# A long-convolution and gated-MLP kernel on one core: two transfers for the first rows, a shorter warm-up, and a new written-out order

## The chip, the cores and the metric

The kernel runs on one core of a Trainium2 chip. The metric is the device time of one execution in microseconds (us). TensorE (PE in the profile, its weight loads PEld), VectorE (DVE), ScalarE (ACT), GpSimd (POOL) and SyncE (SP, which here issues most DMAs) run side by side and wait for each other by semaphores.

## What is computed

All tensors are bfloat16, with 2048 rows of 512 columns. A layer norm of q feeds two branches, whose product is added to q:

```python
x  = A_q
xn = layernorm(x)                       # over the 512 columns
# branch A: shifted k, times v, long convolution over the 2048 rows, times xn
k_shift = sum over t in 0..3 of k_pad[:, t:t+S, :] * shift_k[:, 3-t]
kv = k_shift * v
y  = irfft(rfft(pad(kv)) * rfft(pad(ssm_k)))[:S] + kv * ssm_D
s  = xn * y
# branch B: gated MLP, 512 -> 1792 -> 512
h  = gelu(xn @ w_gate) * (xn @ w_up)
g  = silu(h @ w_down)
return x + s * g
```

## The kernel before

The 2048 rows are 16 tiles of 128 (tile t holds every sixteenth row), and four quarters q of four tiles.

**The MLP.** `ln` (L806 to L818) normalises a quarter: statistics on DVE, a power of -0.5 on POOL, XN written by DVE. `xn_transpose` (L839 for quarters 0 and 1, by matmuls against an identity on PE and copies out of PSUM at L593 or L596; L831 for quarters 2 and 3, by a DMA) makes xnT. `unit(q, m)` multiplies xnT by 128 columns of Wg and of Wu, 14 units to a quarter (matmuls at the helper's L602); ACT applies gelu into GE (L1063, L1072), DVE multiplies into HT (L1065, L1075). The first two units of quarter 0 work in halves of 256 columns, so that they can begin with two of four tiles. Wg and Wu arrive in four parts each, for 2, 4, 4 and 4 of the 14 units (`load_w`). `down(q)` multiplies HT by Wd, 14 matmuls to a tile. In the last quarter ACT applies silu (L1107), DVE multiplies by s and adds x (L1109, L1110), and the tile is stored. The very last tile, t = 15, is cut into two pieces of columns, so that the first is finished while the second is computed.

**The convolution** is a Fourier transform of length 4096 in two stages, by matmuls with tables. The filter ssm_k (Hn) is transposed on PE (L863, f32 view), copied to HTr, multiplied by the table F1 and stored to DRAM (ZH); D is added to one row of HTr (L877). k and v are combined on DVE in four quarters (`kshift`, L940 to L948; the result stands in V), multiplied by F1 and stored (ZK). Both come back as BH and BK for the second stage, whose matmuls are 32x32 tiles (L963). Products of spectra (L1026), the inverse stage (L963, HS and HW with MI), a store (ZI), a load (BI) and a last matmul follow.

**The order.** The program does not run in the order in which it is written down. Each step is a task, with the buffers that it reads and writes; `Sched.run` goes through the tasks in the order of `SEQ`, a list of task numbers written out by hand in the file (a `b` behind a number takes the step's second engine). Every engine executes its share strictly in that order and waits by semaphores for what it needs. `Sched.run` keeps estimated times (`LOAD_NS` for loads, `pe`, `act`, `dve` for the engines), by which it picks free buffers; PSUM has eight banks, of which four may be held by MLP matmuls, four by transposes, and pairs by the convolution. `ORDER` is the order in which load tasks are numbered.

**The start.** `warm_up` issues N_WARM matmuls on a tile of zeros (AST, cleared at L655) into a PSUM bank that nobody reads. SP's queue begins with D (1 KB, L574 like all its copies), four loads of one tile of X each (128 rows of 1 KB per tile), two parts of Hn, Wg's and Wu's first parts, the second quarter of X, Wg's second part, the rows of k that overlap, and so on.

Of the kernel before, what the change touches and what calls it, by code (L numbers as in the profile page):

```python
# [14 lines left out]
DM = 512  # L15
FF = 1792
NT = 16
# [2 lines left out]
NQ = 4  # L20
NG = 32
LN_EPS = 1e-5
TURN = 8192
N_WARM = 22
ORDER = "x00 x01 x02 x03 w0 w1 h0 h1 h2 h3 D0 w2 s0 k0 v0 x1 w3 k1 v1 d0 d1 k2 v2 k3 v3 x2 x3"
SEQ = (
    "28 19 0 2 18 10 3 17 16 4 24 25 11 73 71 1 5 7 6 8 72 50 67 74 79 69 68 20 70 9 21 80 37 75 22 12 82 51 87 81 52 86 32 76 26 23 78 77 54 90 91b "
    "85 89 27 33 84 88 55 367 359 14 53b 356 56 355 357 369 441 439 358 13 363 368 360 361 57 362 379 364 127 381 365 128 440 443 366 442 375 97 377 "
    "98 371 122 444 370 380 59 373 123 61 445 376 446 63 447 58 448 112 15 65 382 450 451 452 378 60b 31 35 34 133 132 134 135 38 383 113 129 384 130 "
    "114 385 115 131 136 449 137 39 30 29 36 45 40 41 372 374 138 62 403 124 407 64 66 386 415 408 125 405 409 99 453 416 395 455 139 410 140 417 418 "  # L30
    "126 100 116 457 459 399 454 456 141 404 102 144 397 47 44 46 42 43 101 460 458 103 401 142 391 400 406 402 145 117 396 119 392 387 393 118 107 "
    "388 398 143 120 389 108 146 390 147 394 104 411 94 485 105 106 413 487 148 465 109 149 412 152 150 414 467 92 110 111 93 95 419 466 477 211 420 "
    "96 212 121 479 216 217 486 218 421 219 422 151 153 488 154 423 155 468 228 461 226 463 227 493 229 156 495 462 429 469 213 434 464 214 157 158 "
    "494 430 221 496 159 160 220 49 230 431 223 222 176 168 215 171 432 224 471 161 162 435 231 505 236 507 433 232 237 83 478 424 233 470 425 163 "
    "234 225 48 235 480 164 165 472 166 481 436 489 238 167 437 491 483 426 490 427 239 473 492 241 475 438 428 630 541 628 539 242 246 474 247 243 "
    "506 248 497 169 170 240 476 629 482 244 542 631 484 245 508 632 634 633 635 636 249 172 499 173 637 174 501 509 498 503 177 500 250 502 513 511 "
    "178 179 515 510 514 641 504 639 638 640 517 181 175 251 182 264 518 183 186 277 180 537 512 516 538 543 540 522 252 544 253b 545 523 546 254 184 "
    "519 256 520 265 255 269 266 549 547 257 548 521 258 532 524 525 527 278 642 185 282 279 290 191 526 267 268 550 533 528 259 262b 260 270 271 529 "
    "534 187 530 263 261 531 188 659 647 535 661 649 651 653 189b 272 275 273 551 655 652 648 280 281 303 190 283 284 285 196 654 650 663 274 657 286 "
    "643 288b 291 536 292b 287 665 295 656 660 658 662 192 644 572 645 193b 646 588 664 194 574 666 293 304 294 296 701 556 589 573 590 308 305 558 "  # L40
    "197 198 199 575 297 591 584 552 195 554 585 298 586 306 299 316 301 592 557 580 307 309 587 559 317 593 201 329 200 206 553 321b 709 555 276 289 "
    "318 582 202 594 203 204 604 319 310 595 596 581 311 300 606 598 302 320 583 322 605 600 568 597 323 607 599 312 314 324 560 564 205 327b 342 602 "
    "325 570 326 328 566 330 334 565 331b 569 576 207 567 571 332 333 578 208 209 562 210 577 691 601 579 335 336 603 561 337 671 713 563 315 340 673 "
    "338b 705 695 618 343 344 693 341 347b 345 346 697 692 619 348 349 608 696 609 698 694 350 339 351 613 683 620 352 353b 354 685 621 313 687 614 "
    "726 715 610 615 707 611 689 616 684 686 622 612 617 623 667 624 668 625 672 669 626 627 674 727 675 716 679 728 670 717 711 699 723 708 729 688 "
    "681 677 718 772 710 680 690 682 676 700 712 678 724 736 730 703 773 719 702 764 714 768 725 770 721 704 743 737 720 738 731 739 744 750 722 706 "
    "757 745 740 732 766 733 774 741 734 769 765 771 746 735 775 767 742 747 751 758 752 753 759 748 754 755 749 760 761 762 756 763 "
)
NF_BANKS = 4
ISSUE = 470.0  # L50
LOAD_NS = {131072: 400.0, 262144: 900.0, 524288: 1300.0, ("h", 524288): 1700.0, ("wg", 524288): 1500.0, ("wu", 524288): 1500.0, 917504: 2620.0, ("sk", 524288): 1900.0, 344064: 1100.0, 46080: 200.0, 3072: 100.0, 1024: 50.0}
W_XT, W_SW, W_BK, W_BH, W_ZI, W_BI, W_ZK, W_MI, W_G1 = 1665000, 600000, 555000, 703000, 333000, 640000, 490000, 740000, 222000
NC_PAIRS = 4
SMALL = 1.15 * 262144
# [235 lines left out]
class Sched:  # L290
# [7 lines left out]
    SHARE_BW = 300.0  # L298
    FIRST = {"loads": 300.0, "SP": 30500.0}
    DRAIN = 121.0  # L300
    EARLY, TAKEN, SHARED, WAIT = (2400.0, 1.3), 1200.0, 46000.0, 3300.0

    def __init__(self):
        self.tasks = []
# [37 lines left out]
    def run(self):  # L342
        free = dict(self.FIRST)
        pipe = 0.0
        order = []
        pmode = 0
        for name in SEQ.split():
            t = self.tasks[int(name.rstrip("b"))]
            eng, dur = t.opts[name[-1] == "b"]
            base = 0.0  # L350
            for d in t.deps:
                base = max(base, d.end + d.lat + (self.SEM if not d.nbytes or t.opts[0][0] != "PE" else 400.0 if d.eng == "loads" else self.HEDGE))
            for b in t.w:
                if b.pool is not None and b.slot is None:
                    f, b.slot = b.pool.find()
                    b.pool.take(b.slot)
                    base = max(base, f + self.SEM)
            t.start, t.eng = max(base, free.get(eng, 800.0)), eng
            free[eng] = t.end = t.start + dur + (self.DRAIN if eng == "PE" and t.mode != pmode else 0.0)
            pmode = t.mode if eng == "PE" else pmode  # L360
            if eng == "loads":
                free[eng] = t.start + dur * (self.EARLY[1] if t.start < self.EARLY[0] else 1.0)
                t.end = free[eng] + self.LOAD_LAT
            elif t.nbytes:
                en = t.end
                if en < self.SHARED:
                    free["loads"] += self.TAKEN
                pipe = max(pipe, en + self.DMA_LAT / 2) + t.nbytes / (self.SHARE_BW if en < self.SHARED else self.DMA_BW)
                t.end = pipe + self.DMA_LAT / 2 + (self.WAIT if en < self.SHARED else 0.0)
            for b in set(t.r + t.w):  # L370
                b.left -= 1
                b.last_end = max(b.last_end, t.end + t.lat)
                if b.left == 0 and b.pool is not None:
                    b.pool.release(b.slot, b.last_end)
            order.append(t)
        assert sorted(t.n for t in order) == list(range(len(self.tasks)))
        return order


def pe(n, cols=512):  # L380
    return n * (cols / 2.4 + 3.0)
# [10 lines left out]
def build_kernel(nc, A_q, A_k, A_v, A_shift_k, A_ssm_k, A_ssm_D, B_w_gate, B_w_up, B_w_down, out):  # L392
    with ExitStack() as es0:
# [19 lines left out]
        X = new("X", [128, NT, DM], BF16)  # L413
# [23 lines left out]
        G = new("G", [128, NT, DM], BF16)  # L437
# [53 lines left out]
        S = Sched()  # L491
        res = trk.res
# [15 lines left out]
        R_X = [res(f"X{t}", X[:, t, :]) for t in range(NT)]  # L508
# [11 lines left out]
        R_GE = [res(f"GE{j}", GE[:, j, :]) for j in range(3)]  # L520
        R_AST = {x: [res(f"AST{x}{j}", a) for j, a in enumerate(ast[x])] for x in "HK"}
        R_G = [res(f"G{t}", G[:, t, :]) for t in range(NT)]
        R_Gh = [res(f"Gh{i}", G[:, NT - 1, 256 * i:256 * i + 256]) for i in range(2)]
        R_HT = [[res(f"HT{j}_{m}", HT[:, j, m, :]) for m in range(MF)] for j in range(2)]
        R_KK = [res(f"KK{t}", KK[:, t, :]) for t in range(19)]
        R_kz = res("kz", KK[0:1, 0:3, :])
# [88 lines left out]
        bWd = [B(f"Wd{i}") for i in range(2)]  # L615
# [43 lines left out]
            for i in range(N_WARM):  # L659
                trk.op("PE", lambda h: mm(h, bank(warm), ZERO[:, 0:128], ZERO, True, True), r=[R_zero], w=R_bank(warm), accum=True)  # L660

        t_warm = S.add([("PE", 10 * 390.0 + (N_WARM - 10) * 220.0)], warm_up, r=[bwarm], w=[warm])
        bcq, bck, bid32 = B("cq"), B("ck"), B("id32")
        S.add([("POOL", 370.0)], lambda e: pool_q(), w=[bcq])
        S.add([("POOL", 1080.0)], lambda e: pool_k(), w=[bck])
# [90 lines left out]
            x_late.append(S.add([("SP", ISSUE)], lambda e: dma(e, args[0], args[1], sem, [], args[2]), w=args[3], nbytes=480000, after=last_load))  # L756

        def load_x0(t, ring):
            load(f"x0_{t}", X[:, t, :], x_dr[:, t, :], R_X[t:t + 1], [bX[0][t]], 131072, ring)

        def load_w(i, rings=("SP", "SP")):
            f0, n = FC[i]
# [315 lines left out]
        def down(q):  # L1078
            for jt in range(4):
                t = 4 * q + jt  # L1080
                cols = [(0, DM)] if t < NT - 1 else [(0, DM // 2), (DM // 2, DM)]
                for c0, c1 in cols:
                    p = B(f"psd{q}_{jt}_{c0}", pF)

# [3 lines left out]
                    for m0, m1 in ((0, 4), (4, 9), (9, 14)):  # L1088
                        def f(e, p=p, jt=jt, m0=m0, m1=m1, pc=pc, c0=c0, c1=c1):
                            for m in range(m0, m1):  # L1090
                                trk.op("PE", lambda h, m=m: mm(h, pc(), HT[:, q % 2, m, 128 * jt:128 * (jt + 1)], Wd[:, m, c0:c1], m == 0, m == MF - 1),
                                       r=[R_HT[q % 2][m], R_Wd[m // 7]], w=R_bank(p), accum=True)
                        down_tasks[q].append(S.add([("PE", pe(m1 - m0, c1 - c0))], f, r=(bHT[q] if jt else bHT[q][m0:m1]) + bWd[m0 // 7:(m1 + 6) // 7],
                                                   w=[p], lat=200.0))
                    n = c1 - c0
                    g, rg = G[:, t, c0:c1], [R_G[t] if n == DM else R_Gh[c0 // n]]
                    bt = B(f"tanh{q}_{jt}")
                    if q < NQ - 1:
                        op([("ACT", act(n))], lambda e, h, g=g, pc=pc: h.activation(g, pc(), ACTF.Tanh, scale=0.5), r=[p], w=[bt],  # L1099
# [122 lines left out]
```

## Time and profile before

| | us |
|---|---|
| median of 3 runs | 198.84 |
| lowest, highest | 198.42, 199.41 |
| the profiled execution | 199.92 |
| its span, first to last instruction | 198.1 |
| PE busy | 192.3 (97% of the span) |
| DVE busy | 159.2 (80%) |
| ACT busy | 122.7 (62%) |
| POOL busy | 12.7 (6%) |

A matmul's busy time overlaps with the next one's, so a PE that is busy throughout still has a pace, which is read from the distance of starts. The span begins with the first instruction and ends with the last; the time of an execution holds some 1.8 us more around it. The chain of waits follows the work that ended last back to its beginning, and at each step names what released it. DMA share is the mean busy share of the 16 DMA engines.

### The profile page before, as it was taken

The page shows a single profiled execution, that of the slowest core. Times are in us where ns is not written, and L with a number is a line of the kernel's source. Part 1 is how long each engine was busy: PE and PEld are TensorE (multiplying, and loading weights), DVE is VectorE, ACT ScalarE, POOL GpSimd, SP SyncE. Part 2 cuts the span into 40 slices and gives each one's busy share as a digit, 9 for nine tenths or more (in the row PEclk, how much of TensorE's full clock was granted, in tenths as well). Part 3 has the DMA queues.
Part 4 walks back from the last instruction along what each step waited for, and adds up shares of the span by engine and source line. Part 5 has one row for each costly group of instructions (what it writes and reads, how often), then busy time and mean ns, then how long its engine had stood idle before and what let it go on. Part 6 is the DMA issues. An engine that isn't in the chain of part 4 may idle for free.

```text
span 198.1 us, 3524 instructions
## 1 busy us (share of the span) xinstructions
PE 192.3 (97%) x1396; PEld 88.2 (45%) x1396; DVE 159.2 (80%) x245; ACT 122.7 (62%) x166; POOL 12.7 (6%) x26
## 2 busy tenths in 40 slices
PE   7998999999999999999999999999999999999993
PEld 2584555444444444444334334434343444444452
DVE  6678898999899995897789796878698815499783
ACT  2587797877883797985667867878654334140031
POOL 6300730000000000020200000000000000000000
PEclk9999999999999999999999999999999999999999
DMA  4999999997759835798999927777512348387406
GB/s 125 346 292 348 366 377 414 416 387 255 303 184 285 294 107 159 237 342 262 311 309 251 378 92 255 265 231 230 192 56 109 106 162 314 113 245 228 160 2 212
DMA packets 34790, 48.14 MB, mean 243 GB/s; under 512 B 8403, under 2 KB 27735, under 8 KB 34774
## 3 DMA queue, kind: packets, MB, share of 16 engines
q1 hardware_dynamic: 29270, 39.53, 61.2%
q10 hardware_dynamic: 5504, 8.39, 11.5%
q8 instruction: 11, 0.18, 0.4%
q14 instruction: 5, 0.04, 0.1%
HBM read 27.39 MB, written 14.68 MB: 212 GB/s over the span
## 4 chain that ended last, share of the span: by engine, by line
PE 90%; DMA 5%; SPq 2%; ACT 1%; DVE 1%; issue 0%
PE psall L602 83%; PE psall L963 5%; DMA Wg<-in_B_w_gate_dram 5%; SPq L574 2%; PE psall L863 1%; ACT HTr L593 1%; PE psall L839 0%; DVE G L1110 0%; DVE G L1109 0%; ACT G L1107 0%
## 5 line engine op out<-in xcount | busy, mean ns | idle before, releaser
L602 PE MATMUL psall<-xnT,Wg 128*128 128x512 bf16 (+1 forms) x232 | 55.6, 372 | 1.0 <-DMA Wg<-in_B_w_gate_dram 1.0
L602 PE MATMUL psall<-xnT,Wu 128*128 128x512 bf16 (+1 forms) x232 | 56.3, 372 | 0.0
L602 PE MATMUL psall<-Wd,HT 128*128 128x512 bf16 (+1 forms) x238 | 53.5, 367 | 0.0
L1075 DVE TENSOR_TENSOR HT<-psall,GE 128x512 bf16<-128x512 f32 x54 | 36.6, 687 | 17.7 <-PE psall L602 16.7
L1072 ACT ACTIVATE GE<-psall 128x512 bf16<-128x512 f32 x54 | 31.1, 600 | 16.9 <-PE psall L602 15.2
L602 PEld LDWEIGHTS psall<-Wd,HT 128*128 128x128 bf16 x238 | 22.8, 98 | 25.6 <-issue 1.3
L602 PEld LDWEIGHTS psall<-xnT,Wg 128*128 128x128 bf16 x232 | 21.8, 98 | 26.9 <-issue 2.2
L602 PEld LDWEIGHTS psall<-xnT,Wu 128*128 128x128 bf16 x232 | 22.0, 98 | 25.3 <-issue 1.8
L593 ACT ACTIVATE HS<-psall 128x1024 bf16<-128x1024 f32 x14 | 13.7, 1021 | 4.9 <-PE psall L963 4.8
L593 ACT ACTIVATE BO<-psall 128x1024 bf16<-128x1024 f32 x11 | 10.9, 1022 | 8.6 <-PE psall L963 8.6
L946 DVE TENSOR_TENSOR KAC<-KAC,KTM 128x2048 bf16<-128x2048 bf16 x12 | 14.6, 1219 | 0.1
L944 DVE TENSOR_TENSOR KTM<-KK,SKB 128x2048 bf16<-128x2048 bf16 x12 | 14.6, 1217 | 0.1
L593 ACT ACTIVATE KB<-psall 128x1024 bf16<-128x1024 f32 x11 | 10.9, 1022 | 4.6 <-PE psall L963 4.6
L593 ACT ACTIVATE AST<-psall 128x1024 bf16<-128x1024 f32 x10 | 10.2, 1025 | 4.5 <-PE psall L602 4.5
L1107 ACT ACTIVATE G<-psall 128x512 bf16<-128x512 f32 (+1 forms) x5 | 2.6, 512 | 15.3 <-PE psall L602 15.3
L806 DVE BATCH_NORM_STATS2 stats<-X 128x6 f32<-128x512 bf16 x16 | 10.4, 681 | 1.6 <-DMA X<-in_A_q_dram 1.6
L1099 ACT ACTIVATE G<-psall 128x512 bf16<-128x512 f32 x12 | 7.2, 597 | 6.9 <-PE psall L602 6.7
L815 POOL TENSOR_TENSOR mv<-mv,NHALF 128x4 f32<-128x4 f32 (+1 forms) x5 | 5.9, 1176 | 82.6 <-DVE mv L814 82.6
L1026 DVE TENSOR_TENSOR HW<-KB,HW 128x1024 bf16<-128x1024 bf16 x16 | 11.0, 685 | 0.0
L1026 DVE TENSOR_TENSOR HS<-KB,HS 128x1024 bf16<-128x1024 bf16 x16 | 10.9, 684 | 0.0
L1101 DVE SCALAR_TENSOR_TENSOR G<-G,psall 128x512 bf16<-128x512 bf16 x12 | 7.9, 681 | 3.2 <-ACT G L1099 3.2
L596 DVE CAST KB<-psall 128x1024 bf16<-128x1024 f32 x5 | 6.1, 1225 | 4.8 <-PE psall L963 4.8
(79 smaller groups left out, 187.3 us busy)
## 6 DMA issues: line engine op xcount, KB each, us to landing
BH<-ZH SPq DMA_DIRECT2D x8, 512.0 KB, 5.5
HW<-HS SPq DMA_DIRECT2D x16, 256.0 KB, 3.5
BK<-ZK SPq DMA_DIRECT2D x8, 512.0 KB, 5.3
ZI<-BO ACTq DMA_DIRECT2D x16, 256.0 KB, 2.6
BI<-ZI SPq DMA_DIRECT2D x8, 512.0 KB, 4.3
ZK<-AST SPq DMA_DIRECT2D x5, 512.0 KB, 2.9
Hn<-in_A_ssm_k_dram SPq DMA_DIRECT2D x4, 512.0 KB, 8.2
KK<-in_A_k_dram SPq DMA_DIRECT2D x4, 512.0 KB, 14.8
```

The lines of the kernel that those rows point to most:

```text
L593: return h.activation(o, i, ACTF.Copy, scale=scale)
L596: return h.tensor_copy(o, i)
L602: return h.matmul(o, lhsT=l, rhs=r, start=st, stop=sp)
L806: t_stats[t] = op([("DVE", 670.0)], lambda e, h, t=t: h.bn_stats(stats[:, t, :], X[:, t, :]), r=[bX[q][t % 4]], w=[bst[t]], rr=[R_X[t]], w ...
L944: op([("DVE", dur)], lambda e, h, j=j, m=m: h.tensor_tensor(KTM[:, m.slot, :, :], kk(j), sk(j), ALU.mult), r=need + [bSKB[j], a], w=[m], r ...
L946: op([("DVE", dur)], lambda e, h, m=m: h.tensor_tensor(KAC[:, a.slot, :, :], KAC[:, a.slot, :, :], KTM[:, m.slot, :, :], ALU.add), r=[m], ...
L963: trk.op("PE", lambda h: h.matmul(ps(s, i)[b, :], lhsT=wt(col)[a, :], rhs=data(col)[a, :], start=n < 16, stop=n >= len(todo) - 16, tile_po ...
L1026: return hd.tensor_tensor(o, flat(KB, kb[h]), o, ALU.mult)
L1072: op([("ACT", act(512))], lambda e, h: h.activation(GE[:, g.slot, :], bank(pg), ACTF.Gelu_apprx_tanh), r=[pg], w=[g], rr=lambda: R_bank(pg ...
L1075: op([("DVE", dve(512, 1))], lambda e, h: h.tensor_tensor(HT[:, q % 2, m, :], bank(pu), GE[:, g.slot, :], ALU.mult), r=[pu, g], w=[bHT[q][m]],
L1099: op([("ACT", act(n))], lambda e, h, g=g, pc=pc: h.activation(g, pc(), ACTF.Tanh, scale=0.5), r=[p], w=[bt], rr=lambda p=p: R_bank(p), ww= ...
L1101: op([("DVE", dve(512, 1))], lambda e, h, g=g, pc=pc: h.scalar_tensor_tensor(out=g, in0=g, scalar=1.0, in1=pc(), op0=ALU.add, op1=ALU.mult ...
```

## The change

Five edits come together.

1. The first quarter of X is loaded in two transfers of two tiles each (256 KB, rows of 2 KB) instead of four of one tile (128 KB, rows of 1 KB). Two load tasks fewer shift all task numbers behind them.
2. `N_WARM` is 12 instead of 22.
3. The estimates of `Sched` change: the load times, the stretch in which early loads are counted longer, the warm-up's time, no semaphore time between PE and PE; and a part of `down` no longer depends on all 14 parts of HT but on those that it reads.
4. The last tile's columns are split at 384 instead of 256.
5. `SEQ` is a new list, by which the engines' orders change throughout. On SP, D goes from the first place to behind Wg's last part; Wu's second part goes ahead of the third Hn; one k goes ahead of Wg's last part; Wd's first half goes ahead of three v and one k. On POOL, the products for F1 and the f32 identity go ahead of the bf16 identity. On PE, matmuls on HTr go between the first ones on Wg and Wu. Quarter 1 is transposed on PE as before.

```diff
+LAST = [(0, 384), (384, 512)]
 TURN = 8192
-N_WARM = 22
-ORDER = "x00 x01 x02 x03 w0 w1 h0 h1 h2 h3 D0 w2 s0 k0 v0 x1 w3 k1 v1 d0 d1 k2 v2 k3 v3 x2 x3"
+N_WARM = 12
+ORDER = "x00 x01 w0 w1 h0 h1 h2 h3 D0 w2 s0 k0 v0 x1 w3 k1 v1 d0 d1 k2 v2 k3 v3 x2 x3"
 SEQ = (
-    "28 19 0 2 18 10 3 17 16 4 24 25 11 73 71 1 5 7 6 8 72 50 67 74 79 69 68 20 70 9 21 80 ..."
+    "16 0 2 17 22 23 18 3 1 19 10 7 35 20 11 30 4 8 21 6 5 65 69 66 67 70 68 73 9 74 71 72 ..."
...
-LOAD_NS = {131072: 400.0, 262144: 900.0, ... 1024: 50.0}
+LOAD_NS = {("x0_", 262144): 600.0, 262144: 900.0, ... 1024: 200.0}
...
-    EARLY, TAKEN, SHARED, WAIT = (2400.0, 1.3), 1200.0, 46000.0, 3300.0
+    EARLY, TAKEN, SHARED, WAIT = (13000.0, 1.3), 1200.0, 46000.0, 3300.0
...
-                base = max(base, d.end + d.lat + (self.SEM if not d.nbytes or t.opts[0][0] != "PE" else 400.0 if d.eng == "loads" else self.HEDGE))
+                base = max(base, d.end if eng == d.eng == "PE" else d.end + d.lat + (self.SEM if not d.nbytes or eng != "PE" else 400.0 if d.eng == "loads" else self.HEDGE))
...
-        t_warm = S.add([("PE", 10 * 390.0 + (N_WARM - 10) * 220.0)], warm_up, r=[bwarm], w=[warm])
+        t_warm = S.add([("PE", N_WARM * 427.0)], warm_up, r=[bwarm], w=[warm])
...
         def load_x0(t, ring):
-            load(f"x0_{t}", X[:, t, :], x_dr[:, t, :], R_X[t:t + 1], [bX[0][t]], 131072, ring)
+            load(f"x0_{t}", X[:, 2 * t:2 * t + 2, :], x_dr[:, 2 * t:2 * t + 2, :], R_X[2 * t:2 * t + 2], bX[0][2 * t:2 * t + 2], 262144, ring)
...
-                cols = [(0, DM)] if t < NT - 1 else [(0, DM // 2), (DM // 2, DM)]
+                cols = [(0, DM)] if t < NT - 1 else LAST
...
-                        down_tasks[q].append(S.add([("PE", pe(m1 - m0, c1 - c0))], f, r=(bHT[q] if jt else bHT[q][m0:m1]) + bWd[m0 // 7:(m1 + 6) // 7],
+                        down_tasks[q].append(S.add([("PE", pe(m1 - m0, c1 - c0))], f, r=bHT[q][m0:m1] + bWd[m0 // 7:(m1 + 6) // 7],
```

## The prediction

> **What bounds the kernel now.** I read the chain of waits first, then the timeline of the first 16 us and of the last 10, then busy time by stretch, then the DMA queue's issues with their time to landing. The chain in order of time, cut to five pieces (start, duration, what):
>
> ```profile
> 5.92 9.60 DMA Wg<-in_B_w_gate_dram
> 15.52 0.14 issue
> 15.65 5.34 PE psall L602 x26
> ...
> 35.81 48.35 PE psall L602 x224
> ...
> 157.95 36.30 PE psall L602 x179
> ```
>
> Behind 15.65 us the chain is nearly all TensorE (PE). 224 matmuls of 512 columns in 48.35 us give a pace of 0.2158 us each. At that pace PE has no slack: the span can only shrink by starting the real work earlier, by closing the few holes before 35 us, or after the last matmul. So I price the whole change as PE work plus one offset S, the first real matmul's start plus all idle of PE.
>
> The timeline of the start:
>
> ```profile
> 1.17 7.70 PE L602 MATMUL psall<-AST 128*128 128x512 bf16 x22 [1.17 <-DVE Q L687]
> 6.70 1.68 PEld L602 LDWEIGHTS psall<-AST 128*128 128x128 bf16 x8 [0.28 <-issue]
> 8.71 1.04 PE L863 MATMUL psall<-ident,Hn 128*128 128x128 f32 x8
> 9.58 0.61 PE L839 MATMUL psall<-ident,XN 128*128 128x128 bf16 x8
> 11.47 1.04 PE L602 MATMUL psall<-xnT,Wg 128*128 128x256 bf16 x8
> 15.65 1.02 PE L602 MATMUL psall<-xnT,Wg 128*128 128x512 bf16 x4 [0.96 <-DMA Wg<-in_B_w_gate_dram]
> ```
>
> The 22 dummies (on AST) hold PE until 8.87. Their weight loads come 0.427 us apart until 6.70, then 8 in 1.68 (0.21 each): PE runs at half speed for 5.5 us, at full speed after it. (The granted clock reads 1.00 all along, so only the durations tell.) The first Hn block was issued at 2.97 and took 4.6 us, so it landed at 7.57 and waited over 1 us for dummies. The last line is PE's longest hole.
>
> Busy time by stretch (last three columns: granted clock, DMA share, GB/s):
>
> ```profile
> 3.00:4.00 1.00, 1.00 (x4) 0.31 (x3) 0.82 (x3) 0.00 (x0) 0.81 (x4) 1.00 0.88 246
> 4.00:5.00 1.00, 1.00 (x4) 0.31 (x3) 0.89 (x4) 0.17 (x1) 0.46 (x1) 1.00 0.86 197
> 6.00:7.00 1.00, 1.00 (x5) 0.32 (x3) 0.97 (x5) 0.99 (x2) 0.50 (x1) 1.00 1.06 385
> ```
>
> While X comes in 1 KB rows the DMA engines are 86 to 88% busy for 197 to 246 GB/s; in 4 KB rows (Hn) they move 385. From here to 47 us they are full, so landings follow from the bytes ahead.
>
> **PE's work, before and after.** From the chain: 738 matmuls of 512 columns x 0.2158 = 159.3; 60 of 256 x 0.1085 = 6.5; 32 f32 transposes x 0.111 = 3.55; 32 of XN x 0.0555 = 1.8; 32 groups of sixteen 32x32 tiles x 0.22 and 48 changes between tile and full matmuls x 0.125 (16 cost 0.36, and the run behind it 0.11 too much) = 13.0. Sum 184.15. The last matmul ends at 187.25 + 7.54 = 194.79, so S = 10.64: 8.71 for the start and 1.93 of holes (0.96 for Wg, 0.34 behind an HTr copy at 24.5, the rest small). The new order has the same instructions, 48 changes too, and the last tile as 14 x 0.1625 (384 columns, between the two rows) + 14 x 0.0555 instead of 28 x 0.1085: 3.05 for 3.04. Its work is 184.15 again. Everything hangs on S and the tail.
>
> **Ten dummies fewer, D later, X in two transfers.** Twelve dummies at 0.427 end at 6.3. They no longer decide; the first Hn block does. D's issue (0.72 to 1.13) leaves the front of SP's queue, so the stream starts 0.41 earlier: landing at 7.16 at the latest if 2 KB rows are no quicker. If they were as quick as Hn's, 512 KB would take 1.44 us (364 GB/s, the mean of 6 to 8 us) instead of 2.36 (222, of 3 to 5): 0.92 more, 6.24. I take half, 6.7, and 0.2 for the wait: PE starts at 6.9 instead of 8.71, **-1.8**. D itself is used by one VectorE (DVE) operation far behind; its 0.35 of issue costs nothing at its new place, where the queue waits for room anyway.
>
> **What is late next.** Normalisation does not get earlier: the first X now lands as 256 KB, near 3.4 instead of 3.33; four statistics of 0.68, their sums, two powers on GpSimd (0.75) and four writes of XN (0.37 apart) end near 9.0, against 9.08. So PE does its first eight Hn transposes until 7.8 and waits for XN until 8.1: **+0.3**. The first Wg matmul needs a copy xnT that stands on ScalarE (ACT) behind two HTr copies of 1.03: 7.55 + 2.06 + 0.6 = 10.2, while PE is done at 9.75 or so: **+0.35**. It starts near 10.25 instead of 11.47. The new order then puts six HTr matmuls and the last 256-column ones (1.73 us) ahead of the first use of Wg's second part, so the hole of 0.96 closes: **-0.96**. That part (landed 15.5) now lands between 14.6 and 15.1 and is wanted at 7.4 (work ahead of it) + 7.55 = 14.95: **+0.15**. The ACT hole of 0.34 I leave in, ACT being full from 10 to 30 us in either order; of 0.6 in small holes I keep 0.2. S = 6.9 + 0.3 + 0.35 + 0.15 + 0.34 + 0.2 = 8.25, which is **-2.4**.
>
> **Do the loads allow it?** Landing now, shifted by 0.4 to 1.0, and for a changed place by 1.4 per 512 KB: Wu's second part 17.3 to 17.9 (it passes one Hn), wanted at 10.5 + 8 = 18.5; the last Hn 20.1 to 20.7 against 13.5 + 8; Wg's last part, behind one more K, 30.7 against 33; Wd's first half (46.5 before, wanted now at 46.3) passes three V and one K and lands some 5 us earlier. Each has 0.6 us or more; earlier than S = 7.5 they bind.
>
> **DVE's supply.** The convolution needs V multiplied on DVE (7 operations of 1.22 per quarter). By summed durations in either order, the third quarter is ready at DVE's 63.7 and wanted at PE's 57.6 (61.6 and 56.5 before). DVE ran 2.9 behind its sum. No stall needs S less that lag to be 6.1 or more; before it was 7.7 with 5.1 needed. Fewer waits at the start (0.93 and 0.91 us for xnT and X go) leave a lag near 1: 7.2. It holds, with 1.1 of slack instead of 2.6.
>
> **The tail.** From the last matmul to the end of DVE took 1.06 us:
>
> ```profile
> 194.82 0.38 ACT L1107 ACTIVATE G<-psall 128x256 bf16<-128x256 f32 x1 [0.16 <-PE psall L602]
> 195.24 0.29 DVE L1109 TENSOR_TENSOR G<-G,XN 128x256 bf16<-128x256 bf16 x1
> 195.56 0.29 DVE L1110 TENSOR_TENSOR G<-G,X 128x256 bf16<-128x256 bf16 x1
> ```
>
> Now 384 columns finish 0.78 before the end; ACT 0.49, DVE twice 0.36 run until 0.5 behind it; then twice 0.23 for 128 columns: 1.0. The store shrinks from 64 KB in 1.6 us to 32 KB in 256 B rows, which no store of this trace has. Between 0.3 less (the 1.6 against 2.1 for 128 KB, again) and 0.5 more; I take nothing. The Trainium skill ("DMA: Bandwidth & Descriptors", Specifications) speaks against this piece: a transfer under 512 B makes the engine read, change and write back. By that rule the store could cost another pass, the upper end or beyond.
>
> **Sum.** -2.4 and nothing in the tail. The profiled execution took 199.92 (span 198.1 and 1.8 around it), 1.1 above the median; its span becomes 195.7, its time 197.5. The same step from 198.84 gives 196.5. What this kernel's runs can tell from no change is about 0.5%, 1 us.
>
> **The rivals.** *The clock stays half.* All twelve dummies are slow ones; full speed came 0.4 us after the place where they now end. If the pause until 6.9 makes the count start over, the 5.5 us of the first line repeat: until 12.4 half the pace is lost, 2.75, of which 0.65 falls into the two waits above. Lost 2.1: -0.3, 198.5. If the sparse first work (waits for XN and xnT) doesn't raise the clock until it is dense, near 15.5, 8.6 / 2 - 0.65 = 3.65 are lost: +1.25, **200.1, slower**. It loses to before from the point where half pace lasts beyond 13.0 (6.9 + 2 x 2.4 + 2 x 0.65). Against it: the hole of 0.96 at 14.7 did not slow the matmuls behind it (four in 1.02 with drain), so a short pause alone does not lower the clock; for it: no row shows the clock rise without 13 dense dummies.
>
> The Trainium skill ("TensorE: Matmul & The Clock Gate", part 1) has a free-running window of some 3.4 us that must be busy, so the moment varies from run to run. By that rule 5.1 us of dummies hold a whole window in half of the cases; in the rest, the window that ends by 8 us is some 85% busy, and one more window at half speed is an estimated 1.7 us: 198.2. This trace's 5.5 us fit it.
>
> *DVE or ACT follows too late.* ACT's order is denser at 10 to 20 us, and V's third quarter stalls if DVE keeps its lag of 2.9: 6.1 - (8.25 - 2.9) = 0.75; as much again on ACT. 198.0. For it: DVE is 96% busy from 26 to 76 us. Against it: DVE loses two of its waits.
>
> *The loads don't move.* Rows of 2 KB are no quicker and only D's 0.41 is won: PE starts at 7.36, S is 8.7, and with 0.5 of waits for loads 9.2: 197.4. This lies in the forecast's own range.
>
> **How the numbers follow.** Forecast 0.68, own range 195.6 (both 0.65 of new waits absent, rows as quick as Hn's) to 197.6. Clock half for one stretch 0.10 (198.5), for long 0.08 (200.1); supply 0.14 (198.0). The range 195.6 to 198.6 leaves out the slow clock and some of each edge. Faster than 197.85: the forecast and a third of the supply case, 0.73; slower than 199.8: the long half clock, 0.08, and unseen stalls of the new order, 0.03; the rest 0.16.
>
> **What would show it.** Right: twelve dummies end by 6.4, first Hn transposes near 6.9 at 0.11 each, first Wg near 10.3, no wait for Wg near 15, last matmul near 192.4, final stores about 3.3 us behind. Wrong: Hn transposes at 0.22; PE waiting for DVE at a matmul on V near 66 us; a wait for Hn or Wu near 18 to 21; the last store over 2.2 us.

## Result and the profile after

The changed kernel took 198.05 us (median of 14 runs, 197.22 to 198.66), the kernel before 199.07 beside it (14 runs, 198.37 to 200.71): a ratio of 0.9938, 95% interval 0.9915 to 0.9962. In a second set it was 197.84 against 200.06, 0.989 (0.9864 to 0.9917). It is faster, but by 1.0 us in the first set where 2.3 were forecast, and 1.55 us above the forecast time; the direction was right, the size was not. In the second set the distance is 2.2 us, but only because the kernel before stood 1.0 us higher there; the changed kernel's own time is the same within 0.2.

The chain of waits of the changed kernel (start, duration, what):

```profile
24.21 16.82 DMA V<-in_A_v_dram
...
41.12 0.10 DVE V L949
...
42.27 1.22 DVE KTM L945
...
46.39 0.70 DVE HT L1076
...
47.13 35.57 PE psall L603 x164
...
159.51 33.05 PE psall L603 x156
```

Before, the chain went from Wg's second part at 15.65 us straight into TensorE. Now it stays off TensorE until 47.13: it comes through a transfer of V, a DVE multiplication on it and a late product HT. The timeline of PE, start and the two holes:

```profile
1.17 4.95 PE L603 MATMUL psall<-AST 128*128 128x512 bf16 x12 [1.17 <-DVE Q L688]
7.03 1.12 PE L864 MATMUL psall<-ident,Hn 128*128 128x128 f32 x8 [0.91 <-DMA Hn<-in_A_ssm_k_dram]
8.48 0.72 PE L840 MATMUL psall<-ident,XN 128*128 128x128 bf16 x8 [0.33 <-DVE XN L819]
10.48 1.04 PE L603 MATMUL psall<-xnT,Wg 128*128 128x256 bf16 x8
...
44.14 1.04 PE L603 MATMUL psall<-xnT,Wg 128*128 128x512 bf16 x4 [0.60 <-DVE HT L1076]
...
47.13 1.04 PE L603 MATMUL psall<-Wd,HT 128*128 128x512 bf16 x4 [0.23 <-DVE HT L1076]
```

The start is near the forecast: the dummies end at 6.12 (6.3 forecast), Hn begins at 7.03 (6.9) and Wg at 10.48 (10.25). Only XN's transposes in between come clearly later, at 8.48 instead of 8.1. The hole at Wg's second part is gone. Without the two new holes (0.77 and 0.39 us by the distance of the matmuls) the offset S would be 8.0; with them it is 9.17: the last matmul ends at 193.32 where 192.4 was expected. DVE's side of the same moment, and the issues on SP's queue that lead to it:

```profile
41.12 1.22 DVE L949 TENSOR_TENSOR V<-KAC,V 128x2048 bf16<-128x2048 bf16 x1 [2.27 <-DMA V<-in_A_v_dram]
```

```profile
23.26 0.43 SPq L575 DMA_DIRECT2D V<-in_A_v_dram  x1
23.73 0.43 SPq L575 DMA_DIRECT2D Wd<-in_B_w_down_dram  x1
24.21 9.04 SPq L575 DMA_DIRECT2D V<-in_A_v_dram  x3
```

The first V issued, at 23.26, is the second quarter, whose multiplication runs only at 54.46; then comes half of Wd; the first quarter is the third in line and lands at 41.03. DVE waits 2.27 us for it, and the HT products behind it in DVE's order come too late for PE. In the kernel before, V's first quarter was the first of its loads:

```profile
22.11 2.58 SPq L574 DMA_DIRECT2D V<-in_A_v_dram  x2
41.21 1.22 DVE L948 TENSOR_TENSOR V<-KAC,V 128x2048 bf16<-128x2048 bf16 x1
```

There it landed 9.4 us behind its issue, at 31.5, and DVE used it at 41.21 without a wait.

The tail, in the timeline of ACT and DVE:

```profile
193.36 0.28 ACT L1108 ACTIVATE G<-psall 128x128 bf16<-128x128 f32 x1 [0.29 <-PE psall L603]
...
194.02 0.22 DVE L1111 TENSOR_TENSOR G<-G,X 128x128 bf16<-128x128 bf16 x1
```

DVE ends 0.92 us behind the last matmul (1.0 forecast, 1.06 before), and the 32 KB store takes 1.5 us against 1.6 for 64 KB.

### The profile page after: what moved, and what is told of

Its sections match the earlier page's. It is cut to its first block, busy times and chain, and to the rows that moved or that the text cites. A ratio compares the mean times of both kernels' runs of the same rounds, so it can differ in the third digit from the quotient of the medians.

```text
span 196.5 us, 3509 instructions
## 1 busy us (share of the span) xinstructions
PE 190.1 (97%) x1386; PEld 86.4 (44%) x1386; DVE 159.3 (81%) x247; ACT 121.3 (62%) x164; POOL 11.6 (6%) x26
## 4 chain that ended last, share of the span: by engine, by line
PE 74%; DMA 11%; SPq 7%; DVE 5%; issue 2%; POOL 0%; ACT 0%; DVEq 0%
PE psall L603 69%; DMA V<-in_A_v_dram 9%; SPq L575 7%; PE psall L964 5%; DMA X<-in_A_q_dram 2%; DVE stats L807 1%; DVE HT L1076 1%; DVE KTM L945 1%; DVE KAC L947 1%; POOL mv L816 0%; DVE xnT L597 0%; DVE HTr L597 0%; DVE G L1111 0%; DVE G L1110 0%; DVE mv L808 0%
## 5 line engine op out<-in xcount | busy, mean ns | idle before, releaser
L603 PE MATMUL psall<-Wd,HT 128*128 128x512 bf16 (+2 forms) x238 | 52.5, 367 | 0.2 <-DVE HT L1076 0.2
L603 PEld LDWEIGHTS psall<-Wd,HT 128*128 128x128 bf16 x238 | 22.2, 98 | 26.5 <-issue 1.3
L594 ACT ACTIVATE HS<-psall 128x1024 bf16<-128x1024 f32 x16 | 15.6, 1021 | 5.3 <-PE psall L964 4.4
L594 ACT ACTIVATE AST<-psall 128x1024 bf16<-128x1024 f32 x12 | 12.1, 1021 | 6.1 <-PE psall L603 5.9
L597 DVE CAST KB<-psall 128x1024 bf16<-128x1024 f32 x7 | 8.6, 1225 | 8.9 <-PE psall L964 8.9
L1100 ACT ACTIVATE G<-psall 128x512 bf16<-128x512 f32 x12 | 7.2, 598 | 10.8 <-PE psall L603 10.2
L594 ACT ACTIVATE KB<-psall 128x1024 bf16<-128x1024 f32 x9 | 9.1, 1023 | 5.1 <-PE psall L964 5.1
L1108 ACT ACTIVATE G<-psall 128x512 bf16<-128x512 f32 (+2 forms) x5 | 2.6, 512 | 14.0 <-PE psall L603 14.0
```

The costliest lines, as they stand in the source:

```text
L594: return h.activation(o, i, ACTF.Copy, scale=scale)
L597: return h.tensor_copy(o, i)
L603: return h.matmul(o, lhsT=l, rhs=r, start=st, stop=sp)
```

## Experiments

All diffs are against the changed kernel unless they say "before". S is the end of the last matmul less 184.15 us, in the profiled execution. The kernel before ran beside them in four sets, at 199.92 us (experiments 1 to 3), 200.06 (4, the first of 5, the first of 7, 9), 198.86 (the second of 7, 10) and 198.88 (8). Its level moved, while the versions with V's first quarter first, 12 dummies and X in two transfers lay at 196.8 to 197.1 in three of the sets. So I compare versions by their own medians and by S; experiment 6 shows where executions of the kernel before differ.

**1. V's first quarter first.** One exchange in `SEQ`: 34 is the load of V's first quarter, 39 of its second.

```diff
-    "39 59b 40 34 122 123 ..."
+    "34 59b 40 39 122 123 ..."
```

> The changed kernel, with the loads of V's first and second quarter exchanged in SP's queue (the first now ahead of Wd's first half); every other instruction stands where it stood. Theory A (V's first quarter, landing at 41.0 us, holds DVE for 2.27 us and through DVE's late products HT holds PE for 0.77 and 0.39 us near 44 and 47): the quarter lands near 36, DVE does not wait, both PE holes go, the last matmul moves from 193.3 to about 192.15, and the time falls by 1.1 us against the changed kernel, to about 0.988 of before. Rival B (the holes come from DVE being too slow for the new order, and the load only happened to be last): a DVE wait of under 0.5 us remains elsewhere and PE still loses 0.7 us or more before 60 us; gain under 0.4 us. Rival C (the size was missed because the profiled execution of before was a slow one): no gain.

Measured 197.11 us (196.78 to 198.60), 0.9865 (0.9832 to 0.9897) of before in its set. S is 8.11, and the chain runs through the place of the two holes:

```profile
8.58 0.72 PE psall L840 x8
...
34.16 8.20 PE psall L603 x38
42.41 13.76 PE psall L603 x63
```

DVE no longer waits for V, PE no longer for HT. The load order is the cause of the holes.

**2. k's second quarter ahead of its third as well** (with V's first quarter first; tasks 42 and 38, the loads of k's third and second quarter, are exchanged too).

```diff
-    "... 28 42 27 26 38 39 59b 40 34 ..."
+    "... 28 38 27 26 42 34 59b 40 39 ..."
```

> As the kernel with V's first quarter early, and k's second quarter exchanged with its third as well (DVE waited 0.39 us for it at 34.7). Theory A: DVE gains 0.4 us more of slack, PE has no hole left there, so the time is the same within 0.2 us as with V alone. Rival B (DVE's supply binds PE): another 0.3 to 0.4 us gained.

Measured 197.05 us (197.01 to 197.18), 0.9852 (0.9826 to 0.9878), S 8.04: the same as experiment 1, so nothing further in DVE's supply binds.

**3. The dummies: 22 in the changed kernel, 12 in the kernel before.**

```diff
-N_WARM = 12
+N_WARM = 22
```

```diff
 before:
-N_WARM = 22
+N_WARM = 12
```

> The changed kernel with 22 dummies instead of 12. They would end near 8.8 and PE starts its real work 1.7 us later than at 7.03. Theory A (behind the start, PE is held at 44 to 47 us by a load whose landing does not depend on PE): most of the 1.7 us is absorbed there, the holes of 0.77 and 0.39 shrink or vanish, and the time is only 0.3 to 0.7 us longer than the changed kernel's. Rival (the start counts in full): 1.7 us longer, slower than before.

> The kernel before with 12 dummies instead of 22, nothing else. PE's first transposes start at Hn's landing, 7.6 instead of 8.71. Theory A (in the old order PE waits at 15.65 for Wg's second part, which lands at 15.5 whatever PE does): the hole of 0.96 grows to about 2 us and the time stays within 0.2 us of before. Rival (the dummies alone carry the gain): 1.0 us faster, 0.995.

The first took 198.11 us (197.30 to 198.73), as the changed kernel, and not 0.3 to 0.7 us more. In its profiled execution (197.50 us, S 8.37) the first Wg matmul comes at 10.73, only 0.25 later than with 12 dummies; DVE waits 1.21 us for V and PE not at all behind it. That the late V hides what 22 dummies cost fits this, but experiment 4 is the cleaner test. The second took 200.49 (198.83 to 201.94), ratio 1.0017 (0.9987 to 1.0046): no gain by itself. The larger hole at Wg's second part that the theory expected did not come either. In its profile the first Hn block landed at 9.1 us, 2.9 behind the dummies:

```profile
9.20 1.93 PE L863 MATMUL psall<-ident,Hn 128*128 128x128 f32 x8 [2.94 <-DMA Hn<-in_A_ssm_k_dram]
```

1.93 us for eight transposes instead of 1.04 is half speed. So with the old load order the shorter warm-up can lose the clock. It did so in most executions: eight of the twelve have a mean granted clock of 0.980 to 0.991 (3.4 us at half speed make 0.991 of 199 us), where the executions of the kernel before beside them have 0.997 or more. The three at 1.000 took 198.83 and twice 199.54 us, less than the 199.92 of the kernel before.

**4. 22 dummies with V's first quarter first.**

```diff
-N_WARM = 12
+N_WARM = 22
-    "39 59b 40 34 122 123 ..."
+    "34 59b 40 39 122 123 ..."
```

> V's first quarter first, and 22 dummies instead of 12. Theory: with this order and these loads it is the chain from X over the statistics to XN, and behind it xnT and Wg, that sets the first Wg matmul, not the dummies; 22 dummies end between 7.6 and 8.9 us, where PE would otherwise do eight Hn transposes and then wait for XN. So first Wg matmul at most 0.3 to 0.9 us later than the 10.58 us with 12 dummies, and the time 0 to 0.5 us above V's first quarter first with 12. Rival (the prediction's sum, in which the ten dummies are the gain): PE starts 1.0 to 1.9 us later and the time is 1.0 to 1.8 us longer.

Measured 197.69 us (197.40 to 198.54), S 8.75. Against experiment 1, measured in another set, that is 0.58 us (0.64 in S): ten dummies fewer are worth about a third of the 1.8 that the forecast gave to the earlier start, just above the theory's 0.5 and far below the rival. The two ratios' intervals (0.9832 to 0.9897, 0.9862 to 0.9917) overlap, so the size is rough.

**5. The changed kernel again.** 

> The changed kernel once more, beside the others on the same chip. If V's first quarter is the whole shortfall, it stands 0.9 to 1.5 us above any version of this set that loads V's first quarter first and begins as early, with DVE waiting some 2.3 us for V near 41 us and PE twice for DVE's HT near 44 and 47 us (1.16 us together in the earlier trace). If the earlier trace was a chance landing, the wait for V is under 0.5 us here and the time is within 0.4 us of the version with V's first quarter first.

> The changed kernel once more, for a profiled execution. Theory: DVE's wait for V's first quarter near 40 us is above 1.6 us where PE has holes behind DVE's HT near 44 and 47 us, and at or below 1.6 us where it has none; the execution is longer by the holes. Expected wait 1.2 to 2.6 us, holes 0 to 1.2 us, and time = 197.5 us plus holes within 0.3 us. Rival: holes of 0.5 us or more without that wait, or none with a wait above 2 us.

The first took 197.84 us (197.01 to 198.39). In its profiled execution (197.50 us) DVE waited 1.65 us for V and PE not at all: S 8.40. In the second (198.02 us) DVE waited 2.41, PE 0.23 twice by the records, and S was 8.90:

```profile
40.35 1.23 DVE L949 TENSOR_TENSOR V<-KAC,V 128x2048 bf16<-128x2048 bf16 x1 [1.65 <-DMA V<-in_A_v_dram]
```

```profile
40.85 1.23 DVE L949 TENSOR_TENSOR V<-KAC,V 128x2048 bf16<-128x2048 bf16 x1 [2.41 <-DMA V<-in_A_v_dram]
```

V's landing differs by 0.8 us between executions of the same kernel. PE's loss by the distance of its matmuls was nothing in the first, 0.8 us in the second and 1.16 in the execution shown above, so it follows the moment at which DVE gets V (40.35, 40.85, 41.12) and not the length of DVE's wait. The first hole ends 3.02 us behind that moment in both executions that have it (43.87, 44.14); 3.02 behind 40.35 is 43.37, and PE came to that matmul only at 43.72. I had expected at least 0.9 us in all executions; it is a stall that some of them escape.

**6. The kernel before again, three executions.** 

> The kernel before, unchanged, for one more profiled execution: its runs gave a median of 199.07 us in one set and 199.92 and 200.06 us in two others. Theory: the differences lie in the start, in when the first Hn block lands against the end of the dummies and in the hole ahead of Wg's second part; everything behind 36 us takes the same time as in the first profile within 0.2 us, and the offset S lies between 9.5 and 11.5 us. Rival: the rest of the kernel is slower there, and the stretch behind 36 us differs by over 0.3 us.

> The kernel before once more, for a profiled execution. Theory: the time of an execution is 184.15 us of PE work, its offset S and 5.1 us of tail and surroundings, and S differs between executions by what happens before 17 us (the moment at which the clock rises in the dummies, which end between 7.4 and 8.9 us, the landing of the first Hn block between 7.5 and 9.2 us, and the hole ahead of Wg's second part). So an execution of 198.0 to 198.6 us has S of 8.8 to 9.4, with PE's first Hn transpose at 7.4 to 8.0 us or no hole at Wg; one of 200 us has S of 10.8, with it at 8.7 or later. Rival: S is the same within 0.3 us in executions whose times differ by 1 us, the difference lying behind 36 us or outside the span.

> As for before_b: a further execution of the kernel before, with the same two theories.

They took 200.40, 198.41 and 199.04 us. The timelines of the first and of the second:

```profile
1.17 6.36 PE L602 MATMUL psall<-AST 128*128 128x512 bf16 x22 [1.17 <-DVE Q L687]
9.23 1.13 PE L863 MATMUL psall<-ident,Hn 128*128 128x128 f32 x8 [1.70 <-DMA Hn<-in_A_ssm_k_dram]
...
16.17 1.02 PE L602 MATMUL psall<-xnT,Wg 128*128 128x512 bf16 x4 [0.86 <-DMA Wg<-in_B_w_gate_dram]
```

```profile
1.17 6.35 PE L602 MATMUL psall<-AST 128*128 128x512 bf16 x22 [1.17 <-DVE Q L687]
7.36 1.04 PE L863 MATMUL psall<-ident,Hn 128*128 128x128 f32 x8
...
14.14 1.02 PE L602 MATMUL psall<-xnT,Wg 128*128 128x512 bf16 x4 [0.80 <-DMA Wg<-in_B_w_gate_dram]
```

With the execution that the prediction read:

| time of the execution | dummies end | first Hn transpose | S | time less last matmul |
|---|---|---|---|---|
| 198.41 | 7.52 | 7.36 | 9.13 | 5.13 |
| 199.04 | 8.55 | 8.38 | 9.79 | 5.10 |
| 199.92 (the prediction's) | 8.87 | 8.71 | 10.64 | 5.13 |
| 200.40 | 7.53 | 9.23 | 11.16 | 5.09 |

(A start may precede a listed end, since ends of matmuls are modelled.) The differences in time are the differences in S, to 0.04 us, and those follow the first Hn transpose to about 0.5. Nothing behind the start differs: from the first matmuls on Wd (47.09 to 49.12 us) to the last run of them (185.74 to 187.77) all four take 138.64 to 138.65 us. The first Hn transpose waits for two things that differ from one execution to the next: the moment at which the dummies go to full speed (22 of them took 6.35 to 7.70 us), and the landing of the first Hn block (by 7.4, or at 9.1). The Trainium skill ("TensorE: Matmul & The Clock Gate", part 1) says that the window behind this clock runs freely, so that the number of slow matmuls changes from run to run; these four executions agree.

**7. X in 1 KB rows, with 12 and with 16 dummies.** Both with V's first quarter first; each of the two load tasks issues two DMAs with semaphores of their own.

```diff
-load(f"x0_{t}", X[:, 2 * t:2 * t + 2, :], x_dr[:, 2 * t:2 * t + 2, :], ..., 262144, ring)
+sems = [dsem(f"d_x0_{t}_{j}") for j in range(2)]
+... for j in range(2): dma(ring, X[:, 2 * t + j, :], x_dr[:, 2 * t + j, :], sems[j], ...)
```

> V's first quarter first, and X's first quarter again in four transfers of 128 KB (1 KB rows), in the same place of the queue; D stays late. Theory (rows of 2 KB land no sooner than rows of 1 KB): the first two tiles land by 3.0 to 3.3 us and the last by 4.9 to 5.4, Hn by 6.6 to 7.2, and the time is within 0.3 us of V's first quarter first. Rival (the 2 KB rows carry a part of the gain, as the prediction counted 0.46 us for them): Hn lands 0.4 us or more later, at 7.3 or behind, and the time is 0.4 us or more longer.

> V's first quarter first, X in 1 KB rows, and 16 dummies instead of 12. With 12 dummies this layout of X had Hn landing at 7.7 us, a pause of 2.04 us behind the dummies, and then Hn and XN transposes at half speed until about 11.5 us (8 Hn transposes in 1.56 us, first Wg matmul at 12.18). Theory (the pause is what keeps the clock at half): 16 dummies end near 7.7 to 7.9 us, close the pause, the Hn transposes behind run at 0.11 each, the first Wg matmul comes at 10.9 to 11.4, and the median is 0.5 to 1.0 us shorter than the 198.64 with 12. Rival (the late Hn block alone costs the time, or the moment of the clock is chance): first Wg matmul at 11.8 or later and the median within 0.3 us of 198.64.

The first took 198.64 us (197.29 to 199.75), 1.5 more than with two transfers: the theory's "within 0.3" was wrong. But rows are not the cause. Four issues take SP 1.82 us instead of 0.87, so Hn is issued at 2.59 instead of 1.64; from issue to landing it takes 5.1 us, against 5.0. X itself is not slower in short rows: from 2 to 4 us the DMA engines move 225 to 311 GB/s, against 188 to 254 in experiment 1, and X's last part lands near 4.3 us instead of 5.4. What follows is a gap in which they have too little to do. The stretch from 4 to 5 us, first in the changed kernel, whose start is that of experiment 1, then here (last columns: DMA share, GB/s):

```profile
4.00:5.00 1.00, 1.00 (x4) 0.31 (x3) 0.46 (x1) 0.98 (x3) 0.77 (x3) 1.00 0.99 254
4.00:5.00 1.00, 1.00 (x4) 0.33 (x3) 1.00 (x4) 0.98 (x3) 0.76 (x3) 1.00 0.43 95
```

PE then waits 2.04 us behind the dummies:

```profile
7.81 1.56 PE L865 MATMUL psall<-ident,Hn 128*128 128x128 f32 x8 [2.04 <-DMA Hn<-in_A_ssm_k_dram]
```

and in the busy times by stretch (third column from the right: granted clock) the clock falls:

```profile
8.00:9.00 1.00, 1.00 (x8) 1.00 (x8) 0.65 (x2) 0.45 (x1) 0.00 (x0) 0.67 1.12 345
9.00:10.00 1.00, 1.00 (x10) 0.94 (x9) 0.16 (x1) 1.00 (x2) 0.00 (x0) 0.50 1.10 384
```

With 16 dummies, which cover most of the pause, Hn lands even later, at 8.0, but runs at full speed:

```profile
8.14 1.13 PE L865 MATMUL psall<-ident,Hn 128*128 128x128 f32 x8 [0.77 <-DMA Hn<-in_A_ssm_k_dram]
```

First Wg matmul at 11.34 instead of 12.18, S 8.93 instead of 9.81, median 198.08 (197.75 to 199.46): 0.56 less. Its ratio, 0.9974 (0.9950 to 0.9997), is worse than the 0.9916 (0.9884 to 0.9949) with 12, but only because before stood 1.2 us lower in that set; the verdict rests on the rows. So of the 1.7 us in S that four transfers cost in these profiled executions (9.81 against 8.11), about 0.9 is the clock and 0.8 the later issue. The clock is lost in only a part of the executions: with 12 dummies three of nine have a mean granted clock of 0.989 to 0.991 (198.64 to 198.95 us, the median among them), four others took 197.29 to 197.84 us, and two, at 0.998, took 199.39 and 199.75 for a reason that no trace shows. With 16 dummies all twelve have 0.997 or more.

**8. Six dummies**, with V's first quarter first (`N_WARM = 6`).

> V's first quarter first, and 6 dummies instead of 12, which end near 3.7 us, 3 us ahead of the first Hn block. Theory (a pause of 2.0 us or more left PE at half speed in two kernels, one of 1.70 or less did not): Hn transposes at 0.22 each, granted clock 0.50 for some 3 us, first Wg matmul near 12 to 12.5 us instead of 10.6, median 1.0 to 2.0 us longer than the 197.11 with 12. Rival (the clock rises with the first dense work whatever was ahead of it): first Wg matmul within 0.4 us of 10.6 and the median within 0.4 us of 197.11.

Measured 198.55 us (197.97 to 199.61), ratio 0.9981 (0.9958 to 1.0003), 1.44 us above experiment 1, as the theory had it:

```profile
6.84 1.94 PE L864 MATMUL psall<-ident,Hn 128*128 128x128 f32 x8 [2.92 <-DMA Hn<-in_A_ssm_k_dram]
```

First Wg matmul at 11.99. Only the granted clock was a miss: in the profiled execution it reads 1.00 throughout, as it does during the slow dummies of every kernel here. It showed half speed where PE paused for 2.04 or 2.94 us behind 12 dummies; where PE had been at half from the beginning, only durations tell.

**9. Statistics of the second tile ahead of the third's** (with V's first quarter first), so that DVE doesn't wait for X's second transfer.

```diff
-    "... 6 5 65 69 66 67 70 68 73 9 74 71 72 ..."
+    "... 6 5 65 67 66 68 73 9 74 69 70 71 72 ..."
```

> V's first quarter first, and DVE computes the statistics of the second tile before those of the third (in the changed order it does tiles 0, 2, 1, and waits 0.86 us for the second transfer while tile 1 has landed). Theory: the first XN comes 0.5 to 0.7 us earlier, PE's wait for XN (0.33 to 0.64 us) closes, but the first Wg matmul moves by only 0 to 0.3 us, since its copy of xnT stands on ACT behind two copies of HTr; time 0 to 0.3 us shorter. Rival (the normalisation's chain alone sets the start): the first Wg matmul 0.5 to 0.7 us earlier and the time 0.5 us or more shorter.

Measured 196.87 us (196.62 to 197.30), 0.9845 (0.9821 to 0.9868). PE's wait for XN is gone, the first Wg matmul comes at 10.11 instead of 10.58, S is 7.66. By the median this is 0.24 us less than experiment 1, measured in another set, and within the theory's 0.3; by S and by the first Wg matmul it is 0.45 and 0.47, a little more.

**10. The same with the split at 256, and with the exchange of k from experiment 2.**

```diff
-LAST = [(0, 384), (384, 512)]
+LAST = [(0, 256), (256, 512)]
```

> V's first quarter first, statistics of the second tile ahead of the third's, and the last tile split at 256 as before. Theory (the tail was counted at nothing): the end of DVE 1.06 instead of 0.92 us behind the last matmul, the last store 64 KB instead of 32, and the median 0 to 0.3 us longer than the 196.87 with the split at 384. Rival (32 KB in 256 B rows is slow to store): 0.2 us or more shorter.

> All corrections together: V's first quarter ahead of its second, the second k behind it, statistics of the second tile ahead of the third's. Theory: the k loads bind nowhere, so this is the same as without the exchange of k, 196.6 to 197.1 us, without a PE wait for DVE's HT near 44 and 47 us. Rival: the exchange closes DVE waits for k that reach PE, and it is 0.3 us or more shorter.

196.82 us (196.63 to 198.19) and 197.03 (196.56 to 198.18): neither can be told from experiment 9 (ratios 0.9914, 0.9888 to 0.9940, and 0.9917, 0.9888 to 0.9945, in a set where before had 198.86). The time from last matmul to the end of the execution is 5.08 us with the split at 256 and 4.97 at 384, so the split is worth 0.1. In the second the early start met a limit that the prediction had named, Wg's last part:

```profile
33.00 1.02 PE L603 MATMUL psall<-xnT,Wg 128*128 128x512 bf16 x4 [0.59 <-DMA Wg<-in_B_w_gate_dram]
```

So the corrections of experiments 1 and 9 give the best version here, 196.9 us, 1.0 below the changed kernel's 197.84 in the same set.

## Why the forecast was too good

In the terms of the prediction, time = 184.15 + S + the rest. The rest is 5.1 us before (experiment 6) and 4.95 after. The medians then give S of 9.8 before (199.07) and 8.95 after (198.05): 0.85 from S and 0.15 from the tail, the 1.0 measured. The prediction had 10.64 and 8.25. Two steps failed.

**"The same step from 198.84 gives 196.5."** The sum was made on an execution at 199.92 and predicted 197.5 for its counterpart, which an execution of the changed kernel without the V stall met to the tenth (197.50, last matmul 192.55), partly by luck: its S was 8.40, 0.15 above the forecast, and its tail 0.15 shorter. Subtracting the whole 2.4 from the median then assumed that what made that execution slower is common to both kernels. It was not: experiment 6 shows it in the very start that the change removes, with S between 9.13 and 11.16. A median execution of before had only 1.5 to win; 1.0 of the error of 1.55 lies here; the other step cost 0.7, of which the tail gave back 0.15. A sign was there: the profiled execution lay above all three runs that the prediction had (198.42 to 199.41). The prediction cited the varying moment of the clock among its rivals and did not carry it into the base of its sum.

**"Do the loads allow it?"** This paragraph followed Wd's first half past three V and one k, and saw only that Wd gains. It didn't ask what V's first quarter loses, and "DVE's supply" looked at the third quarter only. That V's second quarter goes ahead of its first stands neither in the list of the change nor in the prediction. The first took 9.4 us from issue to landing before and 16.8 after, behind 1.4 MB of V and Wd; it is needed at 38.9, landed at 41.0, and costs S up to 1.2 us: 0.8 to 0.9 in the median (8.95 against 8.0 to 8.1 with the quarters exchanged). Wd's half, for which it waited, landed at 39.0 and was used at 47.1. This comes nearest to the rival "DVE or ACT follows too late", by its effect (PE waits for DVE) and its size (198.0), but the cause is another, a load in place of DVE's lag, and so is the quarter. Of the loads that the paragraph did follow, Wg's last part landed at 32.1 instead of 30.7, which left 0.7 us of room in the changed kernel and none in one execution of experiment 10.

**What held.** The start at 6.9 (7.03; 6.78 to 7.05 in three profiled executions), the closed hole at Wg's second part, and the sum: 8.25 forecast, 8.11 once V was in order. The terms inside the sum fared worse, so that it is near is partly luck. XN was ready at 9.74 and not at 9.0: the second X transfer landed at 5.3, and DVE, which takes the tiles in the order 0, 2, 1, waited 0.86 us for it (experiment 9 mends this). By the distance of starts PE waited 0.56 to 0.89 us for XN where 0.3 were counted. The wait for xnT (0.35) did not occur: the copy was ready at 10.17, as forecast (10.2), but PE had transposes to do until 10.47. The holes of 0.15 at Wg's second part and 0.34 behind an HTr copy did not appear either.

Rows of 2 KB were no quicker, as the third rival had it. Hn came earlier all the same, by another way: two issues fewer on SP (experiment 7). Its issue moved by 1.34 us (0.41 for D, 0.93 for the two), its time to landing grew from 4.6 to between 5.0 and 5.3, and the start came out as if half of the 0.92 had been won: the number was right by luck, not by the reason given.

**The clock rivals** did not happen in the change: pauses of 0.9 to 1.4 us behind the twelve dummies left full speed in all three profiled executions. They are real and near. A pause of 1.70 us behind 22 dummies left full speed in before (experiment 6); pauses of 2.04, 2.92 and 2.94 us had half speed behind them, at about 0.9 us (experiment 7) and 1.4 (experiment 8). So the twelve dummies need Hn early: they work with its issue at 1.63 us, lose the clock in some executions at 2.59, and in most with the old queue, at 2.97, where they bring nothing (experiment 3). The edits are not a sum of parts: the two fewer transfers and D's later place bring the Hn block close enough behind the dummies. D's place by itself was not tried.

**The Trainium skill's rule against short rows** ("DMA: Bandwidth & Descriptors", Specifications) did not show at the size that the prediction allowed for: the 32 KB store in 256 B rows took 1.5 us, the 64 KB store in 512 B rows 1.6. Half the bytes had been counted at up to 0.3 less, so a smaller cost of short rows, 0.2 or so, is not ruled out.

**Open.** Why the first Hn block of before lands at 9.1 us in one execution and before 7.4 in another, and why the median of before moved between 198.86 and 200.06 over the sets while the versions with V in order stayed at 196.8 to 197.1. The two sets that ran on one chip gave 198.86 and 198.88, those on two other chips 199.92 and 200.06, so the level may go with the chip; but single executions on the first of these chips took from 198.41 to 200.40, and with so few sets it is not shown. Executions of the single runs in the sets have no trace, so how often before starts late in each is not known.

## What to carry to other kernels

When a transfer is moved ahead in a queue that is full, go through each one that it passes and compare the new landing of that one with its need, first piece first; in a written-out order look also at which piece of a tensor comes first. Before a saving is subtracted from a median, read more than one execution of the kernel before: if the term that the change removes is itself what differs between executions, a median execution has less of it to give. And a shorter warm-up must be judged with the landing of the first real operand, since what counts is the pause between them.

## What the hardware showed that I had not expected

- A pause of TensorE far shorter than the warm-up can lose full speed: 2.04 us did in one execution, 1.70 in another did not, and of nine executions of the kernel with the pause of 2.04 three lost it by the granted clock. The fall came 0.5 us after the pause had ended (a third of 8 to 9 us was still at full speed) in experiment 7 and 0.1 us after it in experiment 3, and lasted 3.4 us in both (until 11.8 and 12.7 us).
- The granted clock does not show the half speed of the first dummies (0.427 us each at a reading of 1.00), only that after a fall (0.50 at 9 to 11 us in experiment 7).
- At the start of the queue the number of issues set the landing: 0.95 us more of issuing on SP put Hn 1.0 us later and left the DMA engines at 0.43 of their time from 4 to 5 us, while X in rows of twice the length did not shorten Hn's 5 us from issue to landing.
- The same 512 KB of V took 9.4 us from issue to landing as the first of its group and 16.8 behind 1.4 MB more (24.21 to 41.03), with 0.8 us of difference between executions.
